# Three weight conversions ordered behind copies of turned attention weights

## The chip, the core and the metric

The program runs on one core of one Trainium2 chip. The metric is the device time of one execution in microseconds (us), smaller is better; the figure quoted is the median of several runs. The engines are TensorE (PE in the profile, its weight loads PEld), VectorE (DVE), ScalarE (ACT), GpSimd (POOL) and SyncE (SP, which here only issues DMA transfers).

## What is computed

Causal attention with a decay bias for 4 batches of 8 heads (576 tokens, head size 64), then a gated layer without nonlinearity, then a layer of eight soft experts:

```
scores = q @ k.T / sqrt(D)  + min(-(cum_i - cum_j), 0), causal
x      = softmax(scores) @ v                # 2304 tokens x 512
h      = ((x @ w1) * (x @ w2)) @ w3 @ w_out # w1, w2: 512 x 1024
logits = h @ phi                            # 32 slots
out    = softmax_slots(logits) @ experts(softmax_tokens(logits).T @ h)
```

The weights w1, w2, w3 and w_out reach the chip as 64-bit floats and are turned into 32-bit floats by the kernel itself.

## The kernel before, in words

**Attention.** The work list of attention has 16 half heads and then 24 whole heads. Item n of the half heads holds either token tiles 0, 1, 2 or token tiles 3, 4 of a head (tile 0 has 64 tokens, the others 128). For each tile, TensorE makes scores (L349), VectorE masks them and finds the extreme value (L352, nmax), ScalarE takes the exponential (L357), GpSimd divides by the sum (L370), TensorE turns the tile (`att_transpose`, L385 into pt_ps, and the diagonal pieces of all tiles of the item, L399 into ptd_ps), and ScalarE copies the turned weights from PSUM to SBUF (L387 into pt, L401 into ptd). The PSUM buffers of pt_ps and ptd_ps are of tag tp, and there are two. For two heads together TensorE then multiplies by the values (`att_pv`, x_ps, one group of matmuls that begins only when the last copies of both items are there), ScalarE and VectorE write x (L434, L435).

**Gate.** `glu_half` multiplies x by one block of w1 or w2 (L447, gl, 12 matmuls). For w1 ScalarE copies the product out (L453, a); for w2 VectorE multiplies the two (L465). The products and the attention's scores share four PSUM buffers of tag sg.

**Conversion.** `load_words` handles half k of the weight list. For w1 and w2 (k = 0 to 15; two halves make the block of one fc) SyncE fetches 512 KB of 64-bit words into one of three buffers raw_w. `convert` begins with one ScalarE instruction (L192, scale the upper words), three VectorE instructions follow (L195, L196, L199), then a ScalarE copy (L223) and a GpSimd subtraction (L224). When L199 has read raw_w, the buffer is free for the fetch of half k + 3.

**Order.** SyncE issues its transfers in the order in which the program is written. For every other engine the instructions are put in order beforehand by a planner that works with its own estimates of time; on the chip, each engine then takes its instructions in that fixed order and waits for what the next one needs. A dependence of class NoSync gives the planner an order and adds no semaphore between engines.

In the fixed order of ScalarE around 60 us stand three conversions (k = 10, 11, 12). Counted by the written order of the program, the copies named in the diff are these: for k = 10 the copy of tile 3 of item 8, for k = 11 that of tile 4 of item 8, for k = 12 that of tile 3 of item 9. In the rows below they are the L387 copies at 60.19, 62.69 and 66.64 us; the three conversions are the L192 instructions at 58.96, 62.12 and 65.92 us.

Of the kernel before, what the change touches and what calls it, by code (L numbers as in the profile page):

```python
# [47 lines left out]
def attn_glu_softmoe_kernel(  # L48
# [31 lines left out]
    def psum(tag, name):  # L80
        return ps.tile([P, 512], F32, tag=tag, name=name, bufs=PB[tag])
# [2 lines left out]
    NW, NRAW, NG4, NX, NE_ = 8, 3, 4, 6, 11  # L84
    NRW, SCB, PTB, QAB, VB = 2, 3, 2, 2, 2
    NF32, NDIR, ND, FAR = 16, 2, 1, 3

    A1, CA, CB1, CB, GB1, GB, GC = 0.6, 8, 16, 26, 8, 16, 24

# [77 lines left out]
        nc.sync.dma_start(rows_d[:, :, :, :, 512:], dec[2])  # L167


    words = {}  # L170
    TODO = [("w12", i) for i in range(FC)] + [("wot", i) for i in range(4)] + [("w3t", i) for i in range(FC)]
    N0 = len(TODO)
    TODO += [("wo", i) for i in range(4)] + [("w3", i) for i in range(FC)]
# [7 lines left out]
    def convert(k, w, by_act, behind=None):  # L181
        raw = words.pop(k)
        pair = raw.bitcast(I32).rearrange("p (n t) -> p n t", t=2)
        hi, lo = pair[:, :, 1], pair[:, :, 0]
        wi, wu = w.bitcast(I32), w.bitcast(U32)
        order = mybir.DependencyInfo(mybir.DependencyClass.NoSync, mybir.DependencyReason.DATA)

        def line_up(step):
            if behind is not None:
                tc.add_manual_dep(step.ins, behind.ins.name, order, reason="order")  # L190

        line_up(nc.scalar.activation(out=w, in_=hi.bitcast(F32), func=AF.Copy, scale=F64_SCALE))  # L192
        lu = lo.bitcast(U32)
        if not by_act:
            nc.vector.tensor_scalar(out=wi, in0=wi, scalar1=3, scalar2=None, op0=ALU.logical_shift_left)  # L195
            nc.vector.scalar_tensor_tensor(  # L196
                out=wi, in0=hi, scalar=-0x80000000, in1=wi, op0=ALU.bitwise_and, op1=ALU.bitwise_or
            )
            return nc.vector.scalar_tensor_tensor(  # L199
                out=wu, in0=lu, scalar=29, in1=wu, op0=ALU.logical_shift_right, op1=ALU.bitwise_or  # L200
            )

        line_up(nc.scalar.activation(out=lo, in_=lu, func=AF.Copy, scale=LO_SCALE, bias=-0.49999))
        nc.vector.scalar_tensor_tensor(  # L204
            out=wi, in0=wi, scalar=3, in1=lo, op0=ALU.logical_shift_left, op1=ALU.bitwise_or
        )
        return nc.vector.scalar_tensor_tensor(
            out=wi, in0=hi, scalar=-0x80000000, in1=wi, op0=ALU.bitwise_and, op1=ALU.bitwise_or
        )
# [4 lines left out]
    def load_words(k, ap):  # L214
        (kind, i), e = TODO[k // 2], k % 2
        span = slice(512 * e, 512 * e + 512)
        if kind == "w12":
            if e == 0:
                w12_t[i] = wp.tile([P, 2, 2, KC, P], F32R, tag="W", name=f"w12t_{i}", bufs=NW)
            w = gq.tile([P, 512], F32, tag="g4", name=f"w_{kind}_{i}_{e}", bufs=NG4)  # L220
            convert(k, w, False)
            th, tl = (w12_t[i][:, n].rearrange("p a k f -> p (a k f)")[:, span] for n in range(2))
            nc.scalar.copy(out=th, in_=w)  # L223
            nc.gpsimd.tensor_tensor(out=tl, in0=w, in1=th.bitcast(F32), op=ALU.subtract)  # L224
        elif k < 2 * N0:
            if e == 0:
                rows_t[kind, i] = gq.tile([P, FC, P], F32, tag="g4", name=f"{kind}_{i}", bufs=NG4)
            rows_w[kind, i] = convert(k, rows_t[kind, i].rearrange("p c f -> p (c f)")[:, span], True)
        else:
            if e == 0:  # L230
                rows_t[kind, i] = ap.tile([P, 1024], F32, tag="words", name=f"w_{kind}_{i}", bufs=NRAW)
            convert(k, rows_t[kind, i][:, span], True, st["a_copy"])
# [141 lines left out]
    def att_transpose(n, i, ap):  # L374
        t = hd[n]
        tiles = [j for j in ITEMS[n][1] if j]
        if i == tiles[0]:
            t["pt"] = ap.tile([P, 10, P], F32, tag="pt", name=f"pt_{n}", bufs=PTB)
            t["ptd"] = ap.tile([P, 5, 64], F32, tag="ptd", name=f"ptd_{n}", bufs=PTB)
        pt, ptd = t["pt"], t["ptd"]  # L380
        W = sum(QT[i])
        sc = t["sc"][:, 64 * i * i : 64 * i * i + W]
        tp = psum("tp", f"pt_ps_{n}_{i}")
        for j in range(i):
            nc.tensor.transpose(tp[:, j * P : (j + 1) * P], sc[:, j * P : (j + 1) * P], ident)  # L385
        p0, step = PT[i]
        t["turned", i] = nc.scalar.copy(  # L387
            out=pt[:, p0 : p0 + step * (i - 1) + 1 : step], in_=tp[:, : i * P].rearrange("p (j q) -> p j q", q=P)
        )
        if i == tiles[-1]:  # L390


            dg = psum("tp", f"ptd_ps_{n}")
            own = [j for j in ITEMS[n][1] if j] + [0] * (ITEMS[n][1][0] == 0)
            for k in [len(own) - 1, *range(len(own) - 2, -1, -1)]:
                j = own[k]
                c0 = max(0, 64 * j * j + sum(QT[j]) - P)
                p0 = 64 * k + (64 if j == 0 else 0)
                nc.tensor.transpose(dg[:, p0 : p0 + P], t["sc"][:, c0 : c0 + P], ident)  # L399
                t["diag", j] = k  # L400
            t["turned", "d"] = nc.scalar.copy(out=ptd[:, : len(own)].rearrange("p j q -> p (j q)"), in_=dg[:, 64 : 64 * len(own) + 64])  # L401

    def att_pv(n, blk):

        b, c = divmod(ITEMS[n][0] // 2, H // 2)
        t0, nt, tiles = BLK[blk]
        acc = psum("acc", f"x_ps_{n}_{blk}")
        products = []

        def add(cols, weights, vs, start, stop):  # L410
            for e in range(2):
                t = hd[n + e]
                products.append((acc[64 * e : 64 * e + 64, cols], vs(t["v"], e), weights(t), start, stop))

        def diag(i, start, stop):
            d0 = sum(QT[i]) - 64 - t0
            add(slice(d0, d0 + 64), lambda t: t["ptd"][:, t["diag", i]], lambda v, e: v[:, 2 * i, e], start, stop)

        if tiles[0] == 0:
            diag(0, True, True)  # L420
        for j in range(tiles[-1]):

            own = [i for i in tiles if i > j]
            p0 = PT[own[0]][0] + PT[own[0]][1] * j
            add(
                slice(QT[own[0]][0] - t0, sum(QT[own[-1]]) - t0),
                lambda t: t["pt"][:, p0 : p0 + len(own)].rearrange("p i q -> p (i q)"),
                lambda v, e: v[:, 2 * j + 1, e], j == 0, False,
            )
        for i in tiles[-2:]:  # L430
            diag(i, False, i == tiles[-1])
        group(products, [hd[n + e]["turned", i] for e in range(2) for i in (tiles[-1], "d")])
        x = x_t[b, blk, c]
        nc.scalar.copy(out=x[:, 0], in_=acc[:, :nt])  # L434
        nc.vector.tensor_tensor(out=x[:, 1], in0=acc[:, :nt], in1=x[:, 0].bitcast(F32), op=ALU.subtract)  # L435
# [311 lines left out]
    with tc.tile_pool(name="att", bufs=1) as ap:  # L747
# [39 lines left out]
        def load(k):  # L787
            i = k // 2 - 1
            if FC <= i < N0:
                (sum_rows if k % 2 else use_rows)(*TODO[i])  # L790
            if k < 2 * N0:
                load_words(k, ap)
            if k + NRAW < 2 * N0:
                fetch_words(k + NRAW, ap)
# [10 lines left out]
        for i in range(N0, len(TODO)):  # L805
            more += [(1, lambda i=i: fetch_later(i)), (1, lambda: None)]
            more += [(1, lambda k=2 * i + e: load_words(k, ap)) for e in range(2)] + [(1, lambda: None)]
# [8 lines left out]
        k = GC - GB  # L816
# [12 lines left out]
    def big(where, name):  # L829
        if where == "w":  # L830
            return wp.tile([P, 2048], F32, tag="W", name=name, bufs=NW)
        if where == "t":
            return tp2.tile([P, 2048], F32, name=name)
        return ep.tile([P, 2048], F32, tag="E", name=name)
# [3 lines left out]
    for i in range(2):  # L838
        t = big("e", f"wo_t{i}").rearrange("p (i c) -> p i c", i=2)
# [3 lines left out]
    for i in range(4):  # L843
        t = big("e", f"w3_t{i}").rearrange("p (i c) -> p i c", i=2)
# [286 lines left out]
```

## Time and profile before

| what | value |
|---|---|
| median of 3 runs | 555.44 us (553.01 to 556.08) |
| the profiled execution | 556.72 us, span 554.9 us |
| TensorE busy | 519.0 us (94% of the span) |
| VectorE, ScalarE, GpSimd busy | 316.0, 311.5, 199.2 us |
| mean granted TensorE clock | 0.977 of full speed |

The span runs from the first to the last instruction; the execution is 1.8 us longer. A high busy share of TensorE alone does not say that each stage is limited by it: the stretches in which it idles or runs at a lower clock are found in the windows and in the timeline.

### The profile page before, as it was taken

The numbers are of one execution on the slowest core, as the hardware profiler recorded it, in microseconds if no ns is written. First come the engines' busy times: TensorE is split into PE (matmuls) and PEld (weight loads), VectorE is DVE, ScalarE is ACT, GpSimd is POOL, SyncE is SP. The second block draws the span as 40 slices with busy tenths as digits, with TensorE's granted clock in tenths as the row PEclk, the third lists the DMA queues.
The fourth block names the chain that finished last, engine by engine and source line by source line (L and its number), as shares of the span: only waits on it lengthen the run. The fifth ranks groups of instructions, "written<-read, shape, count | busy, mean of one in ns | idle before, by whom it ended". The sixth has DMA issues, their size and how long they took to land.

```text
span 554.9 us, 11841 instructions
## 1 busy us (share of the span) xinstructions
PE 519.0 (94%) x4288; PEld 436.2 (79%) x4288; DVE 316.0 (57%) x966; ACT 311.5 (56%) x845; POOL 199.2 (36%) x247
## 2 busy tenths in 40 slices
PE   3899799999889999999999899999999999999993
PEld 2667588888778898999989799898989999853452
DVE  7568677789865383866457677446641311243433
ACT  4576667688876674865687577557743211321222
POOL 5474463628764474343433444334220000000000
PEclk9997979999799999999999999999999999999998
DMA  5766953977572251654657347454403999689977
GB/s 153 246 164 181 284 186 135 305 289 252 180 254 98 77 189 40 206 174 154 194 170 231 128 150 222 130 170 131 153 33 119 406 409 388 238 297 424 420 288 242
DMA packets 38809, 118.03 MB, mean 213 GB/s; under 512 B 4224, under 2 KB 10560, under 8 KB 35296
## 3 DMA queue, kind: packets, MB, share of 16 engines
q1 hardware_dynamic: 36768, 113.60, 59.7%
q10 hardware_dynamic: 1984, 3.69, 2.5%
q8 instruction: 34, 0.56, 0.4%
q14 instruction: 23, 0.19, 0.1%
HBM read 102.11 MB, written 11.60 MB: 205 GB/s over the span
## 4 chain that ended last, share of the span: by engine, by line
PE 74%; DMA 9%; DVE 8%; issue 3%; ACT 2%; SPq 1%; POOL 1%; DVEq 0%; ACTq 0%; POOLq 0%
PE gl L447 33%; PE x_ps L110 8%; PE sc_ps L349 8%; PE pt_ps L385 5%; DMA raw_w<-in_w 4%; PE gn_ps L617 3%; PE o_ps L1032 3%; DMA raw<-in_qk 3%; PE h_ps L994 3%; PE ptd_ps L399 3%; PE z_ps L110 2%; DVE w3t L204 1%; PE lg L110 1%; DVE sc L352 1%; DVE w_w L204 1%
## 5 line engine op out<-in xcount | busy, mean ns | idle before, releaser
L447 PE MATMUL gl<-x,w12t 128*128 128x320 f32 (+1 forms) x1536 | 240.0, 306 | 0.5 <-DVE gT L465 0.3
L447 PEld LDWEIGHTS gl<-x,w12t 128*128 128x128 f32 x1536 | 214.9, 192 | 8.3 <-issue 4.6
L370 POOL TENSOR_SCALAR sc<-sc,rinv 128x64 f32<-128x64 f32 (+4 forms) x160 | 95.8, 615 | 47.5 <-DVE rinv L367 32.9
L357 ACT ACTIVATE sc<-sc,nmax 128x64 f32<-128x64 f32 (+4 forms) x160 | 89.8, 563 | 34.6 <-DVE nmax L352 34.2
L325 POOL TENSOR_TENSOR qa<-raw,qa 64x576 fp32r<-64x576 f32 x24 | 36.4, 1516 | 136.9 <-DVE qa L319 111.3
L352 DVE CUSTOM_DVE_ANT_0 sc<-sc_ps,mask 128x64 f32<-128x64 f32 (+4 forms) x160 | 64.5, 422 | 31.7 <-PE sc_ps L349 28.0
L387 ACT COPY pt<-pt_ps 128x128 f32<-128x128 f32 (+3 forms) x128 | 53.1, 424 | 36.0 <-PE pt_ps L385 21.7
L385 PE MATMUL pt_ps<-ident,sc 128*128 128x128 f32 x320 | 55.8, 285 | 5.8 <-ACT pt L387 2.6
L349 PE MATMUL sc_ps<-qa 128*128 128x64 f32 (+1 forms) x144 | 46.6, 336 | 6.3 <-DVE nmax L352 3.3
L385 PEld LDWEIGHTS pt_ps<-ident,sc 128*128 128x128 f32 x320 | 38.5, 144 | 15.9 <-issue 7.2
L453 ACT COPY a<-gl 128x256 f32<-128x256 f32 (+1 forms) x64 | 25.5, 400 | 43.9 <-PE gl L447 38.0
L110 PE MATMUL x_ps<-pt,v 128*64 128x256 f32 (+1 forms) x384 | 47.6, 361 | 0.0
L349 PE MATMUL sc_ps<-raw 68*128 68x288 f32 (+4 forms) x96 | 35.4, 513 | 11.3 <-DMA raw<-rows 9.6
L349 PE MATMUL sc_ps<-qb 68*128 68x64 f32 (+1 forms) x144 | 44.0, 310 | 0.0
L1003 POOL MEMSET ht<- 128x1024 f32 x2 | 1.9, 954 | 108.0 <-DVE ew L907 99.1
L110 PEld LDWEIGHTS x_ps<-pt,v 128*64 128x64 f32 x384 | 33.1, 142 | 6.8 <-issue 1.3
L322 POOL TENSOR_TENSOR qb<-raw,qa 64x576 fp32r<-64x576 f32 x24 | 37.5, 1564 | 2.2 <-PE gn_ps L617 0.5
L349 PEld LDWEIGHTS sc_ps<-qa 128*128 128x128 f32 x144 | 27.9, 194 | 9.8 <-DVE nmax L352 4.6
L435 DVE TENSOR_TENSOR x<-x_ps,x 128x320 fp32r<-128x320 f32 (+1 forms) x32 | 13.9, 450 | 37.9 <-ACT x L434 37.9
L349 PEld LDWEIGHTS sc_ps<-raw 68*128 68x128 f32 x96 | 21.2, 258 | 16.1 <-issue 12.3
L192 ACT ACTIVATE w_w<-raw_w 128x512 f32<-128x512 f32 x32 | 21.7, 678 | 18.5 <-DMA raw_w<-in_w 18.4
L357 ACT ACTIVATION_READ_ACCUMULATOR sc<-sc,nmax 128x1 f32 x160 | 31.0, 194 | 0.0
(180 smaller groups left out, 782.5 us busy)
## 6 DMA issues: line engine op xcount, KB each, us to landing
ew<-in_ew SPq DMA_DIRECT2D x27, 1024.0 KB
raw_w<-in_w SPq DMA_DIRECT2D x32, 512.0 KB
raw<-in_qk SPq DMA_DIRECT2D x24, 576.0 KB
v<-in_v SPq DMA_DIRECT2D x16, 576.0 KB
raw_w3t<-in_w3t SPq DMA_DIRECT2D x16, 512.0 KB
raw_wot<-in_wot SPq DMA_DIRECT2D x8, 512.0 KB
raw_wo<-in_wo SPq DMA_DIRECT2D x8, 512.0 KB
w_d<-w_w SPq DMA_DIRECT2D x8, 512.0 KB
```

The costliest lines, as they stand in the source:

```text
L110: mm = nc.tensor.matmul(out_, lhs, rhs, start=start, stop=stop)
L192: line_up(nc.scalar.activation(out=w, in_=hi.bitcast(F32), func=AF.Copy, scale=F64_SCALE))
L322: nc.gpsimd.tensor_tensor(out=qb[0:64, 1, :q1], in0=rk[0:64, :q1], in1=qa[0:64, 1, :q1].bitcast(F32), op=ALU.subtract)
L325: nc.gpsimd.tensor_tensor(out=qa[64:, 0, q0:q1], in0=rq[64:, q0:q1], in1=qa[64:, 0, q0:q1].bitcast(F32), op=ALU.subtract)
L349: nc.tensor.matmul(pp[:r, : z - a], x[:, 0, q0 : q0 + r], x[:, 1, a:z], start=x is mul[0], stop=x is mul[-1])
L352: nc.vector.tensor_tensor_reduce(out=sc[:r, a:z], in0=pp[:r, : z - a], in1=hd["mask"][:r, m0 : m0 + z - a], scale=-0.125, scalar=3.0e38 if ...
L357: nc.scalar.activation(out=sc[:r, :W], in_=sc[:r, :W], func=AF.Exp, bias=nmax[:r, i : i + 1], scale=-1.0, accum_out=rsum[:r, i, 0:1],)
L370: nc.gpsimd.tensor_scalar(out=sc, in0=sc, scalar1=rinv[:, i : i + 1], scalar2=1.0, op0=ALU.mult, op1=ALU.mult)
L385: nc.tensor.transpose(tp[:, j * P : (j + 1) * P], sc[:, j * P : (j + 1) * P], ident)
L387: t["turned", i] = nc.scalar.copy(out=pt[:, p0 : p0 + step * (i - 1) + 1 : step], in_=tp[:, : i * P].rearrange("p (j q) -> p j q", q=P))
L447: nc.tensor.matmul(acc[:, :nt], w12_t[fc][:, wi, n, kc], x_t[b, blk, kc][:, xi], start=k == 0, stop=k == 3 * KC - 1)
L453: st["a_copy"] = nc.scalar.copy(out=a_sb[:, :nt], in_=acc[:, :nt])
```

## The change

A list `turned` collects every L387 and L401 copy in the order in which the program writes them. For halves 10, 11 and 12 the first ScalarE instruction of the conversion gets a NoSync dependence on an entry of that list, counted from its end at that point. The helper `convert` already had the argument `behind` for this.

```diff
+    TIE = {10: 6, 11: 5, 12: 6}
...
-    words = {}
+    words, turned = {}, []
...
-            convert(k, w, False)
+            convert(k, w, False, turned[-TIE[k]] if k in TIE else None)
...
         t["turned", i] = nc.scalar.copy(
             out=pt[:, p0 : p0 + step * (i - 1) + 1 : step], in_=tp[:, : i * P].rearrange("p (j q) -> p j q", q=P)
         )
+        turned.append(t["turned", i])
...
             t["turned", "d"] = nc.scalar.copy(out=ptd[:, : len(own)].rearrange("p j q -> p (j q)"), in_=dg[:, 64 : 64 * len(own) + 64])
+            turned.append(t["turned", "d"])
```

## Rows read from the trace of the kernel before

**Rows 1.** The page, part 1: busy us, share of the span, instructions.

```profile
PE 519.0 (94%) x4288; PEld 436.2 (79%) x4288; DVE 316.0 (57%) x966; ACT 311.5 (56%) x845; POOL 199.2 (36%) x247
```

**Rows 2.** The chain that ended last, in time: start us, us, what.

```profile
57.28 8.56 DMA raw_w<-in_w
...
70.22 3.50 PE gl L447 x12
73.72 2.54 PE x_ps L110 x19
...
87.12 1.76 PE gl L447 x12
...
90.90 1.89 PE x_ps L110 x19
```

**Rows 3.** The chain once more, between 100 and 200 us.

```profile
157.44 5.57 DMA raw<-in_qk
```

**Rows 4.** Windows of 2 us: length, busy us (instructions) per engine, clock, DMA.

```profile
62.00:64.00 2.00, 0.60 (x5) 0.63 (x6) 1.49 (x4) 1.88 (x4) 0.14 (x1) 1.00 0.96 353
...
66.00:68.00 2.00, 1.11 (x8) 1.08 (x9) 1.34 (x2) 2.00 (x6) 1.59 (x2) 1.00 0.90 294
...
70.00:72.00 2.00, 2.00 (x8) 1.85 (x8) 1.83 (x7) 1.96 (x5) 0.04 (x1) 0.50 0.35 99
```

**Rows 5.** Timeline of ScalarE, 58 to 71 us: start, us, instruction [idle <-releaser].

```profile
58.96 0.67 ACT L192 ACTIVATE w_w<-raw_w 128x512 f32<-128x512 f32 x1 [1.75 <-DMA raw_w<-in_w]
59.53 0.66 ACT L357 ACTIVATE sc<-sc,nmax 128x448 f32<-128x448 f32 x1
...
60.19 0.46 ACT L387 COPY pt<-pt_ps 128x384 f32<-128x384 f32 x1
60.55 0.42 ACT L434 CAST x<-x_ps 128x320 fp32r<-128x320 f32 x1
62.12 0.66 ACT L192 ACTIVATE w_w<-raw_w 128x512 f32<-128x512 f32 x1 [1.16 <-DMA raw_w<-in_w]
62.69 0.57 ACT L387 COPY pt<-pt_ps 128x512 f32<-128x512 f32 x1
...
63.68 0.78 ACT L357 ACTIVATE sc<-sc,nmax 128x576 f32<-128x576 f32 x1
...
65.92 0.67 ACT L192 ACTIVATE w_w<-raw_w 128x512 f32<-128x512 f32 x1 [1.38 <-DMA raw_w<-in_w]
66.49 0.25 ACT L401 COPY ptd<-ptd_ps 128x128 f32<-128x128 f32 x1
66.64 0.49 ACT L387 COPY pt<-pt_ps 128x384 f32<-128x384 f32 x1
67.01 0.77 ACT L453 COPY a<-gl 128x320 f32<-128x320 f32 x2
...
68.64 0.31 ACT L401 COPY ptd<-ptd_ps 128x128 f32<-128x128 f32 x1
70.04 0.68 ACT L192 ACTIVATE w_w<-raw_w 128x512 f32<-128x512 f32 x1 [1.09 <-DMA raw_w<-in_w]
```

**Rows 6.** Timeline of TensorE, 58 to 70 us.

```profile
58.72 0.66 PE L385 MATMUL pt_ps<-ident,sc 128*128 128x128 f32 x4
...
63.40 0.52 PE L385 MATMUL pt_ps<-ident,sc 128*128 128x128 f32 x3 [1.56 <-ACT pt L387]
...
66.89 0.63 PE L385 MATMUL pt_ps<-ident,sc 128*128 128x128 f32 x4 [1.33 <-ACT ptd L401]
...
67.57 1.60 PE L349 MATMUL sc_ps<-raw 68*128 68x288 f32 x4
69.11 1.11 PE L110 MATMUL x_ps<-pt,v 128*64 128x256 f32 x2
```

**Rows 7.** Timeline of VectorE: the minimum that an exponential waits for.

```profile
57.13 0.08 DVE L352 DVE_READ_ACCUMULATOR2_ANT nmax<- 128x1 f32 x1
```

**Rows 8.** Timeline of SyncE's queue: fetches of two halves.

```profile
62.64 3.45 SPq L178 DMA_DIRECT2D raw_w<-in_w  x2
```

## The prediction

> **What bounds the kernel now.** I read the page's busy times first. TensorE is busy for 519.0 us [rows 1], 94% of the span, so a change to ScalarE's order can win only where TensorE idles, or where its clock is low. The chain that ended last shows where to look: between 57 and 66 us it runs through no engine at all but through a transfer of 8.56 us into raw_w, the 64-bit words of a conversion [rows 2]. The windows then show what that does: TensorE works 0.60 of 2 us at 62 to 64 and 1.11 at 66 to 68, while DMA is busy 0.90 to 0.96 of the time; at 70 to 72 it works throughout but at a granted clock of 0.50, which is the lower of its two levels, 1.2 instead of 2.4 GHz [rows 4]. Before that fall the engine had idled twice, 1.56 us ahead of the turning of item 9's tile 3 and 1.33 us ahead of that of its tile 4; the profile names ScalarE's copies pt and ptd as the releasers [rows 6]. The timeline of ScalarE says why they were late: it stood 1.75, 1.16 and 1.38 us in front of conversions 10, 11 and 12, each time for the landing of raw_w, and the copies stand behind them [rows 5]. From 70.22 us on the chain's long pieces are TensorE's own again [rows 2], so what is won ahead of that point can reach the end.
>
> **The change, part by part.** No instruction, byte or semaphore is added by the diff itself. What moves on ScalarE: conversion 10 goes behind an exponential (59.53) and the copy of item 8's tile 3 (60.19); conversion 11 behind the copy of item 8's tile 4 (62.69); conversion 12 behind item 8's diagonal copy (66.49) and the copy of item 9's tile 3 (66.64) [rows 5]. I take it that the planner leaves the rest in its order.
>
> *Do the conversions themselves come later?* Each waits for its landing anyway, so the question is whether the target is done by then. I replay ScalarE with the start-to-start distances of the rows.
> - The exponential's input is there at 57.13 + 0.08 = 57.21 us [rows 7], and ScalarE is free since 58.96 − 1.75 = 57.21 [rows 5]. Exponential at 57.3, copy of tile 3 0.66 later, at 57.96, and done by 58.42. Conversion 10 lands at 58.96: 0.54 us to spare.
> - Conversion 10 takes 0.57 to the next start, so the cast of x goes from 60.55 to 59.53 and the copy of tile 4, behind the cast's 0.42 us, to 59.95; its tile is turned at 58.72 + 0.66 = 59.38 [rows 6], so it is ready. Done by 59.95 + 0.57 = 60.52; conversion 11 lands at 62.12: 1.6 us to spare.
> - Behind conversion 11 the exponential, which stood at 63.68 with the copy of tile 4 ahead of it, comes that copy earlier, at about 63.2; its 0.78 us end at 64.0, where the diagonal copy begins, and 0.15 later (as 66.64 follows 66.49) the copy of item 9's tile 3, done at about 64.6. Conversion 12 lands at 65.92: 1.3 us to spare.
>
> So the first step of each costs nothing, hidden by the transfer. Without that cover (a landing as soon as the target is reached) each would be late by the instructions put ahead of it: 1.02 us for half 10 (60.55 − 59.53), at most 0.57 for half 11, 0.52 for half 12 (67.01 − 66.49). What hangs on it is the three VectorE steps, the ScalarE copy and the GpSimd subtraction of the half, and the fetch of the half three later, which SyncE issues when the last VectorE step has freed the buffer; the two fetches of halves 13 and 14 are the ones issued from 62.64 on [rows 8], with the rows and q, k transfers of later items behind them on that queue. Nothing of it moves while the landing comes last.
>
> The wait for the landing of half 12 is what all this rests on, and its price is the 8.56 us of the chain's piece [rows 2]. The Trainium skill, page "DMA: Bandwidth & Descriptors", section "Bandwidth", gives 6.15 us of DMA time for 1 MB, so by an estimate from it 512 KB alone would be there some 3 to 4 us after the issue, before 62 us; ScalarE would then hardly wait in front of half 12, and the change would win nothing there. The trace decides otherwise, with 8.56 us and DMA engines 0.90 busy or more in these windows [rows 4].
>
> *What comes earlier.* TensorE's first gap goes: the copy of tile 4 ends at 60.52 instead of 63.26, so the turning of item 9's tile 3 runs on at 61.84 (63.40 − 1.56) and the work up to 65.56 (66.89 − 1.33) is done at 64.0, 1.56 us sooner [rows 6]. The second gap goes mostly: the diagonal copy comes at 64.0 instead of 66.49, and the turning of tile 4 at about 64.4 instead of 66.89, 2.5 us sooner.
>
> *What is late next.* The next scores (67.57) need free buffers of tag sg, and these are held by gate products until ScalarE has copied them out (L453, 67.01) [rows 5, 6]. The group x_ps at 69.11 needs the diagonal copy of item 9, which stands at 68.64 [rows 5, 6]. Both copies still stand behind conversion 12, and this starts at its landing, 65.92, as before. Between its start and 67.01 there now lies only its own 0.57 us: 66.49 instead of 67.01. So x_ps comes 67.01 − 66.49 = 0.52 us earlier, not 2.9, and the two gaps return as one of about 1.9 us (turning and scores bound) in front of the scores and x_ps. Lower bound of the gain: 0 (something else holds x_ps by then). Upper bound without the clock: the planner also lets the two L453 copies pass conversion 12 (their 0.77 us fall away behind it): 0.52 + 0.77 = 1.29 us. Conversion 13 and its wait of 1.09 us at 70.04 [rows 5] are not touched, and TensorE does not wait for what is behind it until much later. I take 0.52, because the diff binds nothing but the three conversions, and the order between the other copies has no reason to change.
>
> *The clock.* The low stretch after 68 us costs more than the gaps: 12 gate matmuls take 3.50 us against 1.76 at full clock, 19 matmuls of x_ps 2.54 against 1.89 [rows 2], together 1.74 + 0.65 = 2.39 us. Before the fall TensorE did turns and scores with gaps of 1.56 and 1.33 us. After the change it works on without a gap until 64, but then come turns, scores and one gap of nearly 2 us, right ahead of the point where the clock fell. I leave the low stretch in the sum, as the nearest rows have it, and take its 2.39 us as the other end.
>
> Sum: the profiled execution would go from 556.72 to 556.2 us. It lies 1.28 us above the median of the runs shown, 555.44; for the median that is **554.9 us**.
>
> **The rivals.**
> 1. *The clock stays up* (TensorE's rearranged work keeps it at the higher level after 68 us). For it: the densest part, the gate matmuls, now joins the work before it without a break. Against: the hold is moved, not removed. Gain 0.52 + 2.39 = 2.91 us, 552.5; with the upper bound of the order 1.29 + 2.39, 551.8.
> 2. *The gain is given back* in the stage where VectorE's conversions of w3 and the transfers set the pace; the chain goes through a q, k transfer of 5.57 us at 157.44 [rows 3]. If that transfer's issue does not move with TensorE, all 0.52 us are gone: 555.4. The same time comes out if the planner had the targets ahead already, which the rows exclude [rows 5].
> 3. *Slower: another low stretch.* The gaps, until now two, stand together in front of x_ps, or the planner, whose whole later order follows from its estimates, leaves a gap of that size in the w3 stage. It decides if such a gap brings a fall where there is none now: one more low stretch costs at least the 2.39 us above, and with the 1.02 us of half 10, should the landing no longer cover it, 3.4. That is 557.3 (with the gain) to 558.8.
>
> **How the numbers follow.** Chances: the hold moves on to the landing of half 12, 0.45; clock stays up 0.29; given back 0.09; slower 0.17. A measurement of this kernel can tell about 0.5%, 2.8 us: below 552.7 is faster, above 558.2 slower. The clock's case lies on either side of that bound by its 2.39, which counts only two runs of matmuls of the stretch, so most of it, 0.25, is faster; 0.05 of the likeliest comes from a better order further on: 0.30. Of the slower case 0.11 lies beyond 558.2, and 0.03 is added for an order that costs more all along: 0.14. The rest, 0.56, is the same. The likeliest's own range is 553.6 to 556.0. The range that leaves out no more than 2 in 10 goes from 551.6 (the clock's case with the upper bound) to 557.5 (the lower end of the slower one).
>
> **What would show it.** Right, if ScalarE has an exponential near 57.3 and the copy of tile 3 near 58, and conversions 10, 11 and 12 still start within 0.3 us of 58.96, 62.12 and 65.92 with the transfer as their releaser; if TensorE's two gaps of 1.56 and 1.33 us are gone, and one of 1.5 to 2 us stands ahead of the scores or of x_ps, released by ScalarE; and if the clock is still 0.50 at about 70 us. Wrong, if the window at 70 to 72 shows full clock (rival 1), if conversion 12 starts well before or after 65.9, so that the landing itself moved, or if the gap before x_ps is not there because the L453 copies passed conversion 12.

## The result, and the profile after

The kernel after takes 558.64 us (median of 20 runs, 555.79 to 560.85), the kernel before beside it 554.37 us (20 runs, 551.27 to 559.70). The ratio is 1.0079, with a 95% interval of 1.0059 to 1.0098: 4.3 us slower, beyond the 0.5% that the prediction took as the bound, and above its range (551.6 to 557.5). The profiled execution took 560.57 us with a span of 558.8. Every ratio here compares only runs within 1.5% of the fastest of the same kernel.

The page, part 1, answers to [rows 1]: of the 3.9 us by which the span is longer than before (554.9), TensorE is busy for 1.7 more and idle for the rest. VectorE is busy for 4.5 more.

```profile
PE 520.7 (93%) x4288; PEld 435.3 (78%) x4288; DVE 320.5 (57%) x966; ACT 311.6 (56%) x845; POOL 198.8 (36%) x247
```

First the place of the change. Timeline of ScalarE after (start, us, instruction, idle time before it and its releaser), to be held against [rows 5]; lines stand one to three further down than before:

```profile
57.70 0.68 ACT L358 ACTIVATE sc<-sc,nmax 128x448 f32<-128x448 f32 x1
...
59.15 0.48 ACT L388 COPY pt<-pt_ps 128x384 f32<-128x384 f32 x1 [0.67 <-PE x_ps L111]
59.52 0.67 ACT L193 ACTIVATE w_w<-raw_w 128x512 f32<-128x512 f32 x1
...
61.60 0.68 ACT L193 ACTIVATE w_w<-raw_w 128x512 f32<-128x512 f32 x1 [0.60 <-DMA raw_w<-in_w]
...
65.39 0.66 ACT L193 ACTIVATE w_w<-raw_w 128x512 f32<-128x512 f32 x1 [1.82 <-DMA raw_w<-in_w]
...
66.47 0.74 ACT L456 COPY a<-gl 128x320 f32<-128x320 f32 x2
...
160.20 0.65 ACT L204 ACTIVATE raw_w3t<-raw_w3t 128x512 int32<-128x512 uint32 x1 [2.95 <-DMA raw_w3t<-in_w3t]
```

The three conversions stand where the diff puts them, and the last two still wait for their landings. Windows of 2 and 4 us after (length, busy us of TensorE, its weight loads, VectorE, ScalarE, GpSimd, then clock and DMA), the first three against [rows 4]:

```profile
62.00:64.00 2.00, 2.00 (x14) 1.61 (x13) 1.79 (x7) 1.57 (x5) 0.00 (x0) 1.00 1.01 378
66.00:68.00 2.00, 1.06 (x5) 0.82 (x5) 1.91 (x4) 2.00 (x7) 1.36 (x1) 1.00 0.67 183
70.00:72.00 2.00, 2.00 (x17) 1.59 (x17) 2.00 (x5) 1.74 (x4) 2.00 (x2) 1.00 0.85 222
...
122.00:124.00 2.00, 0.76 (x5) 0.50 (x5) 2.00 (x5) 1.22 (x5) 0.61 (x1) 1.00 0.86 295
...
158.00:162.00 4.00, 1.25 (x13) 1.11 (x11) 0.53 (x1) 1.80 (x5) 0.00 (x0) 1.00 1.01 378
162.00:166.00 4.00, 3.53 (x31) 3.00 (x29) 3.24 (x7) 3.47 (x9) 2.05 (x2) 0.59 0.61 205
...
316.00:318.00 2.00, 1.80 (x8) 1.76 (x9) 2.00 (x9) 0.42 (x3) 0.00 (x0) 0.59 0.21 86
318.00:320.00 2.00, 2.00 (x11) 2.00 (x10) 0.24 (x2) 1.81 (x7) 0.00 (x0) 0.56 0.98 322
```

At 62 to 64 us TensorE now works throughout, and at 70 to 72 the clock is 1.00. Compared instruction by instruction, TensorE is 2.5 us ahead of the kernel before at 80 to 100 us. The loss is further on. At 122 to 124 us TensorE works 0.76 of 2 us, at 158 to 162 1.25 of 4, and behind that the granted clock is 0.59, most of that window at the lower of its levels, 1.2 instead of 2.4 GHz. By 170 us the kernel is 2 us behind.

Not all of the difference between these two profiles belongs to the change. At 316 to 320 us another 1.6 us go, where the orders are the same: both profiles have a wait of 1.80 us there (for gU, of VectorE), and only in this one does the clock fall behind it (0.59 and 0.56, against 1.00 before). Over the whole execution the clock is on the side of the kernel after, 0.988 against 0.977; the kernel before had low stretches of its own at 68 to 76 and 142 to 150 us. What the change costs is therefore taken from many runs below, and not from this pair.

What the diff does not show is that the planner made a new order. TensorE's order differs from before in 412 places of the 3440 instructions that the program names, VectorE's in 134 of 774, ScalarE's in 133 of 708, GpSimd's in 20 of 243, all between 57 and 200 us; from there the orders are the same. Timeline of TensorE after:

```profile
66.94 0.75 PE L350 MATMUL sc_ps<-raw 68*128 68x288 f32 x2 [1.37 <-ACT a L456]
...
68.05 0.65 PE L111 MATMUL x_ps<-pt,v 128*64 128x256 f32 x2
...
101.29 0.65 PE L111 MATMUL x_ps<-pt,v 128*64 128x256 f32 x2
101.87 0.62 PE L111 MATMUL wot_ps<-wot,phi_sb 128*32 128x256 f32 x2
102.42 0.65 PE L111 MATMUL x_ps<-pt,v 128*64 128x256 f32 x4
103.00 0.62 PE L111 MATMUL wot_ps<-wot,phi_sb 128*32 128x256 f32 x2
...
123.61 1.34 PE L450 MATMUL gl<-x,w12t 128*128 128x256 f32 x9 [1.24 <-DVE gC L468]
...
161.27 0.77 PE L401 MATMUL ptd_ps<-ident,sc 128*128 128x128 f32 x5 [2.75 <-ACT pt L388]
```

and of the kernel before at the same work:

```profile
104.09 0.65 PE L110 MATMUL x_ps<-pt,v 128*64 128x256 f32 x2
104.67 0.64 PE L110 MATMUL wot_ps<-wot,phi_sb 128*32 128x256 f32 x8
...
105.73 1.51 PE L110 MATMUL x_ps<-pt,v 128*64 128x256 f32 x12
...
107.62 0.98 PE L385 MATMUL pt_ps<-ident,sc 128*128 128x128 f32 x7
...
122.51 1.73 PE L110 MATMUL x_ps<-pt,v 128*64 128x256 f32 x16
124.08 0.40 PE L110 MATMUL x_ps<-ptd,v 128*64 128x64 f32 x8
...
125.25 1.24 PE L447 MATMUL gl<-x,w12t 128*128 128x256 f32 x9
```

Three places are to be seen. Before, the wot_ps (matmuls of w_out's words with phi, 32 columns wide) run together (8 records, 0.64 us); after, they stand in pairs between the x_ps. Before, 24 records of x_ps run at 122.5 while VectorE makes the product gC that frees the buffer for the next gl; after, gl stands in front of them and TensorE waits 1.24 us for gC with nothing to do. And at 161 us ScalarE stands 2.95 us in front of a w3t conversion, with copies pt queued behind it for which TensorE waits 2.75 us.

In this profile the lead itself is lost at the q, k transfer of [rows 3]; the chain after:

```profile
154.38 8.69 DMA raw<-in_qk
```

The transfer is issued 3.06 us earlier than before (154.38 against 157.44) and lands at 163.07, against 157.44 + 5.57 = 163.01.

### The profile page after: what moved, and what is told of

Its sections match the earlier page's. It is cut to its first block, busy times and chain, and to the rows that moved or that the text cites. A ratio compares the mean times of both kernels' runs of the same rounds, so it can differ in the third digit from the quotient of the medians.

```text
span 558.8 us, 11853 instructions
## 1 busy us (share of the span) xinstructions
PE 520.7 (93%) x4288; PEld 435.3 (78%) x4288; DVE 320.5 (57%) x966; ACT 311.6 (56%) x845; POOL 198.8 (36%) x247
## 4 chain that ended last, share of the span: by engine, by line
PE 64%; DVE 3%; DMA 3%; issue 1%; ACT 1%; SPq 0%; DVEq 0%; ACTq 0%
PE gl L450 29%; PE x_ps L111 6%; PE sc_ps L350 5%; PE pt_ps L386 4%; PE gn_ps L620 3%; PE o_ps L1035 3%; PE h_ps L997 3%; PE z_ps L111 2%; PE ptd_ps L401 2%; DMA raw<-in_qk 2%; PE lg L111 1%; DMA raw_w<-in_w 1%; PE y_ps L921 1%; DMA out<-ot 1%; PE out_ps L1059 1%
## 5 line engine op out<-in xcount | busy, mean ns | idle before, releaser
L371 POOL TENSOR_SCALAR sc<-sc,rinv 128x64 f32<-128x64 f32 (+4 forms) x160 | 94.0, 606 | 56.8 <-DVE rinv L368 31.1
```

The costliest lines, as they stand in the source:

```text
L371: nc.gpsimd.tensor_scalar(out=sc, in0=sc, scalar1=rinv[:, i : i + 1], scalar2=1.0, op0=ALU.mult, op1=ALU.mult)
```

## The experiments

Theory 1: the moves gain or do nothing, and the new order behind them costs. Theory 2: the three moved conversions cost, through later weights. Theory 3: only chance falls of the clock differ. To part them, the order of each engine was written out as a list of instruction numbers, each tied to the one before it without a semaphore:

```python
    pin = mybir.DependencyInfo(mybir.DependencyClass.NoSync, mybir.DependencyReason.DATA)
    for text in ORDER.values():
        names = [f"I-{n}" for n in text.split()]
        for a, b in zip(names, names[1:]):
            tc.add_manual_dep(nc.get_inst_by_name(b), a, pin, reason="pin")
```

ORDER covers the stretch in which the two kernels differ. In the traces of runs 1 to 16 lines stand 63 further down than before (scores L412, gl L510, gC L528). Ratios are to the kernel before, run beside each on the same chip, with 95% intervals.

**1. The moves alone, in the old order.**

```diff
 ORDER["ACT"]    # 761, 818, 879: first steps of halves 10, 11, 12
-599 761 698 682 620 818 688 765 734 879 692 748 661
+599 698 682 761 620 688 818 765 734 692 748 879 661
```

> The order of the instructions of TensorE, VectorE, ScalarE and GpSimd as it is before, written out, with one difference: the first steps of the conversions of halves 10, 11 and 12 stand behind the three copies that the change names. Nothing else is moved. Theory 1 (the moves gain, and what costs is the new order that the planner gave to the 150 us behind them): 0.5 to 3 us faster than before, 551 to 554 us. Theory 2 (the three later conversions themselves cost, through later weights): 2 to 5 us slower than before, 556 to 559 us. Theory 3 (only the clock's chance falls differ): no difference beyond the spread of the runs, within 0.2%.

Measured: 1.0022 [0.9987, 1.0057]. The moves cost nothing that can be told, and gain nothing either; theory 1's 0.5 to 3 us are not there. Of theory 2's 2 to 5 us the interval, which ends at 3.2, leaves the lower part; run 3, which has the moves as well, ends at 1.7 us, and with it theory 2 is out.

**2. The new order without the tie.**

```diff
-TIE = {10: 6, 11: 5, 12: 6}
+ORDER = the order of the kernel after
```

> The order of the kernel after on all four engines, written out, without the tie to the copies. Theory 1 (the order is all there is): as the kernel after, 1.006 to 1.010 of before, 557 to 560 us. A rival (the tie adds waits of its own beside the order): clearly faster than the kernel after, by 1 us or more.

Measured: 1.0065 [1.0028, 1.0101]. The order alone makes the loss, in other executions than those of the kernel after; a chance of single runs would not come back, so theory 3 is out as well.

**3 and 4. New order, then old; and the other way.**

```diff
-ORDER = the order of the kernel before
+ORDER = after's order up to 99.5 us, then before's     # 3
+ORDER = before's order for the same work, then after's # 4
```

> The order of the kernel after up to 99.5 us of its trace (the three moved conversions and the re-planned instructions around them), and from there the order of the kernel before. Theory 1: the lead of about 2.5 us that the kernel after has at 100 us stays at least in part, 551 to 554.5 us; all of it may go at the landing of the q and k rows, then 554 to 555. Theory 2 (the moves cost): 556 to 559 us, as the kernel after. Theory 3: within 0.2% of before.

> The order of the kernel before up to 102 us, the three conversions where they were, and from there the order of the kernel after. Theory 1: the loss without the gain, 2 to 5 us more than the kernel after less what a hidden transfer takes up: 558 to 562 us. Theory 2 (the moves cost, the later order does not): as before, 553 to 555.5 us. Theory 3: within 0.2% of before.

Measured: 0.9992 [0.9954, 1.0030] for 3, 1.0060 [1.0026, 1.0094] for 4. The place of the change and its surroundings are worth nothing at the end; everything is lost behind 99.5 us. That the lead of 2.5 us was not kept has the reason given below (it came from the one execution of the kernel before that it was measured against, not from the new order).

**5 and 6. Which part of the later order.**

```diff
+ORDER = before's, but after's from 99.5 to 135 us      # 5
+ORDER = before's up to 135 us, then after's            # 6
```

> The order of the kernel before, except for the instructions that the kernel after starts between 99.5 and 135 us of its trace, which stand in the order of the kernel after. Theory A (the loss is in this middle part, w_out's turned sums among the x_ps and the gaps at 120 to 135 us, and is not won back): 1.004 to 1.008 of before, about 556 to 558.5 us. Theory B (what this part loses is swallowed by the landing of the q and k rows at 163 us, and the loss is in the part behind): within 0.3% of before.

> The order of the kernel before up to the instructions that the kernel after starts at 135 us of its trace, and from there the order of the kernel after. Theory A (the loss is in the middle part): within 0.3% of before. Theory B (the loss is in the w3 stage behind 135 us, where the conversions of w3t on ScalarE stand in front of copies of turned weights): 1.004 to 1.008 of before, about 556 to 558.5 us.

Measured: 1.0064 [1.0030, 1.0098] for 5, 1.0021 [0.9991, 1.0051] for 6. Theory A: the middle part, 35 us long, carries the loss. The two intervals overlap a little, but the 12 runs of each, on one chip, have means of 558.6 and 556.0 us, a difference of 2.6 with an interval of 0.9 to 4.3. The wait of 2.75 us at 161 us, the longest in the trace but for one of 9.60 at its start, is in the late part and costs half a per cent at most. One reading is that TensorE waits there for work that the q, k transfer would have held up in any case; no run shows it.

**7. The wot_ps in pairs among the x_ps, in the old order.**

```diff
 ORDER["PE"]     # 1148 to 1151: wot_ps; 1133 to 1144: x_ps of block 12
-1133 1148 1149 1150 1151 1261 1262 1134 1135 1136 1137 1138
+1261 1262 1133 1148 1134 1135 1149 1136 1150 1137 1151 1138
```

> The order of the kernel before with one change on TensorE: the 4 wot_ps matmuls of the first half of w_out's first chunk stand one by one among the first x_ps matmuls of block 12, as in the kernel after, and no longer together. In the traces the 12 x_ps and 4 wot_ps take 5.5 us in the kernel after and some 3.0 us in before. Theory A (matmuls of the two sums don't run side by side): 2 to 2.5 us are lost in this place, and 0 to 2.5 us of it is left at the end, 554 to 556.5 us. Rival (the 5.5 us are waits for their inputs, not the order): nothing lost in this place.

Measured: 1.0008 [0.9974, 1.0042]. In its place the price is as expected. Timeline of TensorE, with the next chunk's wot_ps, which stay together, for comparison:

```profile
101.11 0.65 PE L173 MATMUL x_ps<-pt,v 128*64 128x256 f32 x2
101.69 0.62 PE L173 MATMUL wot_ps<-wot,phi_sb 128*32 128x256 f32 x2
...
106.64 0.98 PE L448 MATMUL pt_ps<-ident,sc 128*128 128x128 f32 x7
...
110.20 0.64 PE L173 MATMUL wot_ps<-wot,phi_sb 128*32 128x256 f32 x8
```

Two records take as long as eight. From the first x_ps to the next pt_ps it is 5.53 us (101.11 to 106.64), against 3.53 before (104.09 to 107.62, with two gl in it). At the end nothing of it can be measured, but the interval leaves room for up to 2.3 us; that a wait further on takes it up is a reading that no run shows.

**8. The wot_ps together again, in the new order.**

```diff
 ORDER["PE"]
-1133 1148 1134 1135 1149 1136 1150 1137 1151 1138
+1133 1148 1149 1150 1151 1134 1135 1136 1137 1138
```

> The order of the kernel after with one change on TensorE: the 4 wot_ps matmuls stand together again behind the first x_ps matmul. Theory A: 1.5 to 2.5 us are won in this place; if all of it is left at the end, 555 to 557 us, 1.003 to 1.005 of before; if the waits at 122 to 163 us take it up, as the kernel after, 1.006 to 1.008. Rival (the 5.5 us are waits for inputs): nothing won in this place.

Measured: 1.0144 [1.0094, 1.0194], a miss of both: no faster than the kernel after, and rather slower. Timeline of TensorE of this kernel, and then of VectorE in the kernel after:

```profile
108.67 0.41 PE L412 MATMUL sc_ps<-qa 128*128 128x320 f32 x1 [2.24 <-DVE gC L528]
```

```profile
104.70 1.89 DVE L208 SCALAR_TENSOR_TENSOR wot<-raw_wot,wot 128x512 int32<-128x512 int32 x1
...
106.87 1.55 DVE L205 SCALAR_TENSOR_TENSOR wot<-wot,raw_wot 128x512 int32<-128x512 int32 x1
108.45 1.04 DVE L208 SCALAR_TENSOR_TENSOR wot<-raw_wot,wot 128x512 int32<-128x512 int32 x1
109.41 0.48 DVE L468 TENSOR_TENSOR gC<-gl,a 128x320 f32<-128x320 f32 x1
```

The pairs had filled a wait: in the new order VectorE makes gC behind all steps of w_out's chunk. Faster matmuls only arrive at it sooner. That accounts for a gain that is missing, not for a loss; what goes with the loss in these runs is the clock. The one run of this kernel with a mean clock of 0.995 took 555.79 us; the other three of the compared runs, at 0.973 to 0.985, took 561.36 to 562.52.

**9 to 12. Three places together.** They are the pairs of wot_ps, gC of half 5 behind the last two steps of w_out's chunk, and gl in front of the x_ps of block 14.

```diff
+before's order with the three places of after put in                       # 9
+after's order with the three places put back                               # 10
+after's order with the 12 x_ps in front of the 9 gl put back               # 11
+after's order with wot_ps together and gC in front of the two steps        # 12
```

> The order of the kernel before with three places of the kernel after put into it: the 4 wot_ps matmuls one by one among the x_ps of block 12, VectorE's product gC of half 5 behind the two last steps of w_out's turned chunk, and the 9 gl matmuls of the next block in front of the 12 x_ps of block 14 at 122 us. Theory A (these three places are the loss of the middle part): 1.004 to 1.008 of before, 556 to 559 us, and an idle time of TensorE of about 1.2 us behind gC near 122 us. Rival (the loss is spread over the whole middle part, with the clock's falls that follow): within 0.3% of before.

> The order of the kernel after with the same three places put back as they are in before. Theory A: 0.998 to 1.003 of before, 553 to 556 us, at most one idle time over 1 us between 100 and 135 us on TensorE. Rival (spread over the whole middle part): 1.005 to 1.008, as the kernel after.

> The order of the kernel after with one place put back: the 12 x_ps of block 14 in front of the 9 gl matmuls at 122 us, so that they run while gC is made. Theory A: the idle time of 1.23 us at 122 us is gone, 0.8 to 1.5 us less than the kernel after, 1.004 to 1.006 of before, 556 to 558 us. Rival: the wait only moves, as the kernel after (1.006 to 1.008).

> The order of the kernel after with two places put back: the 4 wot_ps matmuls together, and gC of half 5 in front of the two last steps of w_out's turned chunk on VectorE. Theory A (the matmuls one by one only hid a wait for gC that the new order of VectorE makes): the wait of 2.24 us at 106 us that appeared when the 4 were put together alone is gone, and the time is 1 to 3 us below the kernel after, 555 to 557.5 us, 1.002 to 1.005 of before. Rival: as when the 4 were put together alone, 559 us or more.

Measured: 1.0095 [1.0058, 1.0131], 1.0129 [1.0082, 1.0176], 1.0143 [1.0101, 1.0186] and 1.0119 [1.0069, 1.0168]. The first is a little above theory A's 1.004 to 1.008: the three places are enough for the loss. The other three fall: put back in the new order they win nothing. Timeline of TensorE of kernel 10:

```profile
108.29 0.63 PE L328 MATMUL wots_ps<-rep,wotp 128*128 128x32 f32 x4 [0.65 <-ACT wotp L320]
110.38 0.69 PE L462 MATMUL ptd_ps<-ident,sc 128*128 128x128 f32 x2 [0.64 <-ACT pt L450]
```

New waits stand there, now for ScalarE, whose order still is the new one. One reading, which runs 13 to 15 bear out, is that the engines' orders fit each other, and a patch on one or two of them breaks the fit.

**13 to 15. One engine's new order.**

```diff
+before's order; the middle part of TensorE as after                # 13
+before's order; the middle part of VectorE as after                # 14
+after's order in the middle part, TensorE's as before              # 15
```

> The order of the kernel before on all engines but TensorE, and on TensorE the order of the kernel after for what the kernel after starts between 99.5 and 135 us. Theory P (TensorE's new order makes the loss, by matmuls that lose their company and by waits that nothing covers): 1.004 to 1.010 of before, 556 to 559.5 us. Theory V (the new order of VectorE and ScalarE makes it): within 0.3% of before.

> The same for VectorE alone: its order of the kernel after for the middle part, the other engines as before. Theory P: within 0.3% of before. Theory V: 1.003 to 1.008 of before, with waits of TensorE for gC of 1 us or more that the kernel before does not have between 100 and 135 us.

> The order of the kernel after in the middle part on VectorE, ScalarE and GpSimd, and TensorE's order as before. Theory P: within 0.3% of before, 552 to 556 us. Theory V: 1.004 to 1.010 of before.

Measured: 1.0248 [1.0199, 1.0298], 1.0140 [1.0107, 1.0173] and 1.0221 [1.0177, 1.0265], all worse than the whole (1.0064). Neither theory P nor V holds by itself: no engine carries the loss alone, and mixed orders wait for each other. ScalarE's new order alone was not tried. Timeline of TensorE of kernel 14:

```profile
109.66 0.41 PE L412 MATMUL sc_ps<-qa 128*128 128x320 f32 x1 [2.14 <-DVE gC L528]
126.00 0.63 PE L328 MATMUL wots_ps<-rep,wotp 128*128 128x32 f32 x4 [1.21 <-DVE u_sb L329]
130.99 0.64 PE L173 MATMUL w3t_ps<-w3t,u_sb 128*32 128x128 f32 x16 [2.23 <-DVE u_sb L329]
```

**16. One place alone.**

```diff
 ORDER["PE"]     # 1421 to 1432: x_ps of block 14; 1496 to 1504: gl
-1421 ... 1432 1451 1452 1491 1492 1496 ... 1504 1516 1517
+1491 1492 1496 ... 1504 1516 1517 1421 ... 1432 1451 1452
```

> The order of the kernel before with one place changed on TensorE: the 9 gl matmuls of the next block stand in front of the 12 x_ps of block 14 at 122 us, as in the kernel after, so that they wait for gC of half 7 with nothing to cover it. Theory P: an idle time of TensorE of 1.1 to 1.3 us at 122 us; 1 to 2.5 us slower at the end, 1.002 to 1.005 of before. Rival (the landing of the q and k rows takes it up): within 0.15% of before.

Measured: 1.0084 [1.0051, 1.0117]. Timeline of TensorE:

```profile
119.72 0.42 PE L412 MATMUL sc_ps<-qa 128*128 128x320 f32 x1 [0.67 <-DVE nmax L415]
...
121.51 1.33 PE L510 MATMUL gl<-x,w12t 128*128 128x256 f32 x9 [1.22 <-DVE gC L528]
...
123.17 1.74 PE L173 MATMUL x_ps<-pt,v 128*64 128x256 f32 x16
```

The wait is there to the hundredth (1.22 against 1.24 in the kernel after), with one of 0.67 ahead of it, since the scores lost the same cover. Together 1.89 us, but the loss is 0.84% of 554, 4.7 us, above theory P's 1 to 2.5. The clock is lower as well: the mean granted clock of this kernel's 10 runs is 0.985, that of the 15 runs of before beside it 0.992. That the clock makes the rest is not shown.

**17 and 18. One tie at a time, the planner free.**

```diff
-TIE = {10: 6, 11: 5, 12: 6}
+TIE = {12: 6}      # 17
+TIE = {10: 6}      # 18
```

> The change with its third tie alone: the first step of half 12 behind the copy of item 9's tile 3. The planner gives 276 places of TensorE's order another instruction than before, the matmuls of w_out's sums one by one among the x_ps among them, but the 12 x_ps of block 14 stay in front of the 9 gl matmuls at 122 us and gC of half 5 in front of the two last steps of w_out's chunk. Theory C (the loss needs a wait of TensorE that loses its cover, as gl in front of x_ps does): within 0.3% of before, 553 to 556 us. Rival (any order that the planner makes anew over so long a stretch costs): 1.004 to 1.010, 556.5 to 560 us.

> The change with its first tie alone: the first step of half 10 behind the copy of item 8's tile 3. The planner's order differs from that of before in 23 places on TensorE, all before 70 us, and is the same from there. Theory C: within 0.3% of before. Rival (the moved conversion itself costs): 1.003 or more.

Measured: 1.0083 [1.0050, 1.0116] for 17, 1.0020 [0.9981, 1.0059] for 18. In 18 TensorE's order is the old one behind 70 us, and the time is not to be told from the old one. Theory C misses 17: the x_ps still cover gC, yet the long new order loses as much. The timeline of TensorE in 17 has its longest wait, but for the one at its start, elsewhere:

```profile
142.63 0.41 PE L350 MATMUL sc_ps<-qa 128*128 128x320 f32 x1 [2.58 <-DVE nmax L353]
```

Before, the wait in that place is 1.13 us. Which of the 276 places make the loss of run 17 was not tried.

## Why the prediction was wrong

**The step that failed** is "I take it that the planner leaves the rest in its order", with its reason that "the order between the other copies has no reason to change". A tie moves no instruction; it changes what the planner sees as ready, and later choices can follow from that (one tie alone changed 23 places of TensorE's order in run 18, 276 in run 17). 412 places of TensorE's order changed, and runs 2, 4 and 5 (1.0065, 1.0060, 1.0064) show that those between 99.5 and 135 us make the loss, while runs 1, 3, 6 and 18 (0.9992 to 1.0022), in which this part stays as it was, are not to be told from the kernel before. Of the rivals it was the third, in its second form (the planner leaves a gap further on, and the clock falls), given 0.17 and 557.3 to 558.8 us; measured 558.64. Its place was off: the gaps that count are in the stage of w_out and the first of w3, not the later one. Its price, one fall of the clock (2.39 us) and 1.02 us for conversion 10, is not what the runs show either, so that the time lies within its bounds is in part luck.

**The conversions.** Right that they cost nothing that can be told (runs 1 and 3). But the starts were given to 0.3 us, and none kept to it. Conversion 10 came 0.56 us later than before (59.52 against 58.96), because its target, the copy at 59.15 that was put near 58, stood behind an exponential at 57.70 (put at 57.3) and then waited 0.67 us for TensorE, which the replay of ScalarE had left out; 11 and 12 came 0.5 us earlier, with their landings.

**The two gaps** are gone and one of 1.37 us stands in front of the scores, released by the copies of gate products, as the prediction put it, a little shorter than its 1.5 to 2 us. x_ps came at 68.05 instead of 69.11, 1.06 us earlier where 0.52 were taken. The clock did not fall: rival 1, in this place, and by the prediction's own sign (full clock at 70 to 72 us) its likeliest case was wrong there too.

**But the whole gain was priced from one execution.** In kernel 16 the order is that of before up to 119 us, and its profile shows something else than [rows 4 to 6]. Timeline of ScalarE, conversions 10 to 13, and a window:

```profile
58.77 0.66 ACT L255 ACTIVATE w_w<-raw_w 128x512 f32<-128x512 f32 x1 [3.02 <-DMA raw_w<-in_w]
60.66 0.70 ACT L255 ACTIVATE w_w<-raw_w 128x512 f32<-128x512 f32 x1
63.08 0.68 ACT L255 ACTIVATE w_w<-raw_w 128x512 f32<-128x512 f32 x1
66.50 0.68 ACT L255 ACTIVATE w_w<-raw_w 128x512 f32<-128x512 f32 x1 [0.21 <-DMA raw_w<-in_w]
```

```profile
70.00:72.00 2.00, 2.00 (x24) 1.86 (x21) 2.00 (x5) 0.92 (x3) 0.88 (x1) 1.00 0.83 260
```

One wait of 3.02 us in front of conversion 10, none in front of 11 and 12, and no fall of the clock. Where the landings fall, and so the gaps of 1.56 and 1.33 us and the 2.39 us of the low stretch, differs between executions of one order. The other profiles say the same. Nine kernels have the order of before up to 99.5 us or further (runs 4 to 7, 9 and 13 to 16). With the matmul records of each kind matched in order, all nine are ahead of the profile of before at 95 us, by 1.7 to 6.1 us, and none shows a low clock at 70 to 76 (run 13 has one at 64 to 69). The eight with the three conversions moved and the new order up to there, or the moves alone (the kernel after, runs 1 to 3, 8 and 10 to 12), are ahead by 1.0 to 4.3. So the low stretch that the prediction left in its sum, and the lead of 2.5 us, belong to one execution, and runs 1 and 3 gain nothing because there was nothing regular to gain. The size of the likeliest gain, 0.52 us, would not have been seen either way.

**Given back at the q, k transfer** (rival 2): in the profile, yes; the lead was lost at a landing that hardly moved (163.07 against 163.01). It need not be: in the profile of run 1, with the moves in the old order, the lead passes that place (2.7 us at 157, 3.5 at 172).

**What stays open.** One place is enough for the loss (run 16), but run 17 loses without it and run 11 does not win by putting it back, so no single wait is shown as the cause in the kernel after; that it is the fit of the orders is a reading. How much of the 4.3 us is waits and how much clock is not parted by an experiment. Over the compared runs of the 20 kernels, each against its own kernel's mean, 0.01 of mean clock goes with 3.4 us; the mean is 0.987 over the 20 runs of the kernel after and 0.991 over the 112 of the kernel before beside runs 1 to 18, so by this estimate about 1.4 us would be clock. No version was faster than the kernel before by more than the noise.

## What to carry to other kernels

Where a planner sets the order, a tie is a change to the whole order behind it: compare the planned orders first, and price that, not the instructions named. To find out what such a change is worth by itself, write the old order out and move only what was meant. And before a gap is priced, look whether a second execution of the same kernel has it: gaps behind a DMA landing moved by microseconds here while the order stayed the same.

## What the runs showed of the hardware

Matmuls of 32 columns ran side by side only as neighbours: 8 records of wot_ps took 0.64 us together and 0.62 us for every 2 when x_ps of 64 columns stood between (runs 7 and 8). The Trainium skill, page "TensorE: Matmul & The Clock Gate", section "Why this matters for your kernels", gives a gain of 2.38 for three such column tiles at once. The rows agree that neighbours gain, four taking the time of one here, and show that it ends where x_ps stand between them.

VectorE's steps on w_out's words, 0.69 us at 101 us, took 1.89, 1.55 and 1.04 us at 104.7 to 109.4 us in the kernel after. Each time an instruction of GpSimd had begun before and was still running. Timeline of VectorE and GpSimd after:

```profile
100.98 0.69 DVE L208 SCALAR_TENSOR_TENSOR wot<-raw_wot,wot 128x512 int32<-128x512 int32 x1
```

```profile
104.55 1.50 POOL L326 TENSOR_TENSOR qa<-raw,qa 64x576 fp32r<-64x576 f32 x1 [4.75 <-DVE qa L320]
106.12 1.75 POOL L323 TENSOR_TENSOR qb<-raw,qa 64x576 fp32r<-64x576 f32 x1
107.85 2.25 POOL L371 TENSOR_SCALAR sc<-sc,rinv 128x448 f32<-128x448 f32 x2
```

Over the whole trace, the 66 steps of this operation on 128x512 beside which no GpSimd instruction ran took 0.67 to 0.75 us; of the 65 that ran beside one for 0.3 us or more, 34 took over 1.0, up to 2.75. The Trainium skill, page "SBUF — State Buffer", section "Summary: rules for kernel authors", says that a VectorE operation with two SBUF inputs and a GpSimd operation that reads SBUF block each other, the later one until the first is done. The rows fit it, but no run here took GpSimd's work away.
